# Keys of the last 1024 tokens in the second attention as Strassen products, with the token product's block sums moved later

## Chip, cores and metric

The kernel runs on one core of a Trainium2 chip. The metric is the device time in microseconds of one execution. TensorE is called PE below, VectorE DVE, ScalarE ACT, GpSimd POOL, and SyncE, whose queue issues most of the DMAs, SP.

## What is computed

Two kinds of layers alternate, twice, each with a residual connection: linear attention (A) and a gated feed-forward (B).

```python
x = x + A(layernorm(x)); x = x + B(layernorm(x))     # then both once more, same weights
# A: 2048 tokens, width D = 1024, 32 heads of 32
q, k, v = split(x @ wqkv)
phi = lambda t: where(t > 0, t + 1, exp(t)) + 1e-6
kv  = einsum("bhsd,bhse->bhde", phi(k), v)
den = einsum("bhqd,bhd->bhq", phi(q), phi(k).sum(s)) + 1e-6
o   = (einsum("bhqd,bhde->bhqe", phi(q), kv) / den) @ wo
# B: F = 3584
out = (relu(x @ W_gate) * (x @ W_up)) @ W_down
```

## The kernel before

**Tokens and quarters.** The 2048 tokens are 16 tiles of 128 (`ST`), in four quarters of `QT` = 4 tiles; `NS` = 8 tiles are one half. A layernormed tile is transposed by DMA into `xnT[l, quarter]`, which feeds the projections. Matmuls are 128 by 128 by 512.

**Projections.** A unit (`k_unit`, `q_unit`) makes one tile's keys or queries in one half of the columns: 8 matmuls into a PSUM bank, then `phi`: two ACT operations (L407, L408) and a DVE join (L411) that reads the bank. A POOL operation (`k_sum`, L484) adds the finished keys onto a running sum.

**The token product.** The values are never computed token by token. `m_products` makes M = layernormed tokens, transposed, times phi(k), a 1024 by 1024 matrix summed over the tokens, and multiplies it by wv per head afterwards. It uses Strassen's method in Winograd's form: tokens and columns are halved, and seven products of 32 matmuls (four groups `j` of 8) take the place of eight. PE's order is `mx`, `mx`, `mv`, `my`, `mv`, `my`, `my`. The first two need no sums. The others need block sums of token blocks (`n1` to `n4`) and key blocks (`k1` to `k4`), each eight times, once for a pair of tiles; they are DVE operations of 128 by 512, all recorded at L516. The third product reads n1 and k1, the fourth n2 and k2, the fifth n4, the sixth n3 and k3, the last k4. After each group of the fourth product DVE adds two banks (L563, called the V adds here), and the fifth product accumulates on the result. n4 and k4 overwrite blocks that the second product reads.

In the first attention all 64 sums stand inside `m_products`, four to a tick. In the second, k1 to k3 follow each key tile of the last 1024 tokens, n1 to n3 each layernorm of such a tile, and n4 and k4 stand after the second product.

**The normaliser.** After the second product two matmuls with ones (L492) spread the key sum over the partitions. Then a chain per query tile runs: a POOL multiply (L684), a DVE reduce, add and reciprocal (L689 to L691), a POOL scale (L696), a DMA transpose of the queries. It starts 2 ticks after the second product in the second attention, 6 in the first, and steps every 2 or 3 ticks:

```python
later.at(2 if l else 6, lambda: z_chain(0))
...
V += [self.ps.tile([P, NW], F32, tag="a", name=f"mv{j}") for j in range(QT)]
```

**Query blocks.** The second attention's queries of the first 1024 tokens are Strassen products already (`q_blocks`, L641): 28 matmuls of seven 4-matmul products for a block of two tiles by both column halves, where the units would take 32. Each block is cut into four steps, and key units stand between them. The weight sums they need were made in the feed-forward before (`load_q`, `sums_q`) and put into DRAM (`tq`); the token sums come from `sums_x` (L1006 to L1009). Product 1 starts bank X, which is copied to Y; product 5 goes to a bank of `kvp` and is copied to an SBUF tile V; product 2 finishes X, product 6 adds to Y, and Z and V are sums of Y and V; 7, 3 and 4 finish the rest. Each of the four results goes through `phi`.

**Order of the work.** `_Later` counts ticks, one for each unit, step or product group, and runs helpers when they are due; that sets their place in program order. Most instructions are then ordered by a scheduler at compile time. In a stretch marked `manual_schedule`, which includes `m_products`, DVE and POOL keep program order. `LN_AT` holds the ticks of the layernorms of tiles 8 to 15. `_Ring` loads weights in a planned order (`plan_A`) through SP's queue. PSUM has four banks "a" (`ps`), two "b" (`ps3`) and two of `kvp`; weights, slabs, transposed tokens and the like share 16 SBUF buffers.

Of the kernel before, what the change touches and what calls it, by code (L numbers as in the profile page):

```python
# [14 lines left out]
P = 128  # L15
# [4 lines left out]

LN_AT = (4, 8, 12, 16, 32, 35, 38, 41)

# [70 lines left out]
class _Net:  # L93
    def __init__(self, tc, ctx, x_d, wqkv_d, wo_d, wg_d, wu_d, wd_d, out_d):
# [34 lines left out]
        self.td = self.spill.tile([P, self.U, 4, NW], F16, name="td")  # L129
        self.tq = [self.spill.tile([P, 8, NW], F16, name=f"tq{h}") for h in range(2)]  # L130
        self.later = _Later()
# [98 lines left out]
    def xn_home(self, layer, t):  # L230

        low = lambda t: self.x[t][:, 0:self.D // 2].bitcast(BF16)
        if layer == 0:
            h = low(t)
        elif t == 0:
            h = self.temp([P, self.D], BF16, name=f"xn{layer}_0")
        elif t < self.NS:

            h = low(t - 1)
        else:  # L240
            h = self.slab_of(layer, 2 * (t - self.NS))
        self.xn[layer, t] = h
        return h

    def pk_home(self, layer, t):
        if (layer, t) not in self.pk:
            if layer == 0:
                h = self.slab_of(layer, t)
            elif t < self.NS:
                h = self.xb[t]  # L250
            else:
                h = self.slab_of(layer, 2 * (t - self.NS) + 1)
            self.pk[layer, t] = h
        return self.pk[layer, t]
# [170 lines left out]
    def plan_A(self, l):  # L425
        D = self.D
        cols = {"k0": D, "k1": D + NW, "v0": 2 * D, "v1": 2 * D + NW, "q0": 0, "q1": NW}
        for n in ("k0", "k1", "v0", "q0", "q1", "v1", "o0", "o1") if l == 0 else (
                "k0", "k1", "q0", "q1", "t0", "t1", "v0", "v1", "o0", "o1"):
            if n[0] == "t":  # L430
                self.ring.add((l, n), lambda t, h=int(n[1]): self.nc.sync.dma_start(
                    out=t[:, :, :].bitcast(F16), in_=self.tq[h]))
            elif n[0] == "o":
                c = NW * int(n[1])
                self.ring.add((l, n), self.wo_v[:, :, c:c + NW])
            else:
                self.ring.add((l, n), self.wqkv_v[:, :, cols[n]:cols[n] + NW])

    def layer_A(self, l, last_ln):
# [30 lines left out]
        def k_unit(q, j, c, between=None):  # L470
# [3 lines left out]
            later.at(1 + (10 if self.phi_lag else 0), lambda: k_sum(t, slice(c * NW, (c + 1) * NW)))  # L474
            if l and t >= self.NS and c == H - 1:
                later.at(3, lambda: sums(t - self.NS, k1, k2, k3))

# [48 lines left out]

        def sums(i, *fs):
            for f in fs:
                f(i)

        def m_products(q_first):
# [7 lines left out]
            last_k = self.last_phi  # L539
            if l == 0:  # L540
                jobs = [(f, i) for fs in ((n1, k1), (n2, k2), (n3, k3), (n4,), (k4,))
                        for i in range(NS) for f in fs]
                for n, (f, i) in enumerate(jobs):
                    later.at(1 + n // 4, lambda f=f, i=i: self.behind(last_k, f, (i,)))

# [26 lines left out]
            V += [self.ps.tile([P, NW], F32, tag="a", name=f"mv{j}") for j in range(QT)]  # L572
            if l:
                for i in range(NS):
                    later.at(1 + i // 2, lambda i=i: sums(i, n4, k4))
            product(lambda i: part(i, 0), lambda i: part(i, 2), V, True, keep)
# [42 lines left out]

        def q_blocks():  # L620


            xa, xb = self.xnT[l, 0], self.xnT[l, 1]
            sa, sb = self.xs[l, 0]
            q0, q1, t0, t1 = (ring.get((l, n)) for n in ("q0", "q1", "t0", "t1"))
            t0, t1 = (t[:, :, :].bitcast(F16) for t in (t0, t1))
            A = {1: xa[:, 0:4], 2: xa[:, 4:8], 3: sb[:, 4:8], 4: xb[:, 4:8], 5: sa[:, 0:4],
                 6: sa[:, 4:8], 7: sb[:, 0:4]}
            B = {1: q0[:, 0:4], 2: q0[:, 4:8], 3: q1[:, 4:8], 4: t1[:, 0:4], 5: t0[:, 0:4],
                 6: t1[:, 4:8], 7: t0[:, 4:8]}  # L630
            for sc in range(2):
                a = self.slot(f"pq{l}_{sc}", [P, QT, D])
                for i in range(QT):
                    pq_of[sc, i] = a[:, i, :]

            def steps(j):
# [8 lines left out]
                def one():  # L645
                    S["X"] = self.ps.tile([P, NW], F32, tag="a", name=f"qx{j}")
                    mm(1, S["X"], True)
                    S["Y"] = self.ps3.tile([P, NW], F32, tag="b", name=f"qy{j}")
                    nc.scalar.activation(out=S["Y"], in_=S["X"], func=ACT.Copy)
                    v = self.kvp.tile([P, NW], F32, tag=f"kv{j % 2}", name=f"qv{j}")  # L650
                    mm(5, v, True)
                    S["V"] = self.temp(name="qm5")
                    nc.scalar.activation(out=S["V"], in_=v, func=ACT.Copy)

                def two():
                    mm(2, S["X"])
                    self.phi(S["X"], half(pq_of[0, j], 0))
                    mm(6, S["Y"])
# [3 lines left out]
                def three():  # L662
                    mm(7, S["Y"])
                    nc.vector.tensor_tensor(out=S["V"], in0=S["Y"], in1=S["V"], op=ALU.add)
                    self.phi(S["V"], half(pq_of[1, j], 1))
                    mm(3, S["Z"])
                    self.phi(S["Z"], half(pq_of[0, j], 1))

                def four():
                    mm(4, S["Y"])  # L670
                    self.phi(S["Y"], half(pq_of[1, j], 0))

# [158 lines left out]
        else:  # L831
            ring.load_to(ring.index((l, "t1")) + 1)
            for j in range(QT):
                later.at(1 + j, lambda j=j: self.sums_x(l, 0, j))
        for i in range(QT if l == 0 else self.NS, self.ST):
            at = 8 + 3 * (i - QT) if l == 0 else LN_AT[i - self.NS]
            self.ln_at(at, l, i, 2)
            if l:
                later.at(at + 2, lambda i=i: self.send_away(i))
                later.at(at + 8, lambda i=i: sums(i - self.NS, n1, n2, n3))  # L840
        if l == 0:
# [13 lines left out]
        else:  # L855
            run(first)
            k = iter(row_major(k_unit, 1) + row_major(k_unit, 2)[:1])
            Q = q_blocks()
            todo = [Q[0][0]]
            for j in range(QT):  # L860
                todo += [next(k), Q[j][1], next(k), Q[j][2], Q[j + 1][0] if j + 1 < QT else next(k), Q[j][3]]
            run(todo)
            run(row_major(k_unit, 2)[1:], row_major(q_unit, 2))
        for q in range(1, self.NQ - 1) if l == 0 else ():
# [3 lines left out]
            run(row_major(k_unit, q), row_major(q_unit, q))  # L868
        run(row_major(k_unit, self.NQ - 1))
        with self.tc.manual_schedule(engines={mybir.EngineType.DVE, mybir.EngineType.Pool}):  # L870
# [102 lines left out]

    def load_q(self):

        self.wq = [self.slot(f"wq{h}", [P, 2, 4, NW]) for h in range(2)]
        for h, t in enumerate(self.wq):
            for n in range(2):
                self.nc.sync.dma_start(out=t[:, n, :, :], in_=self.wqkv_v[:, 4 * h:4 * h + 4, n * NW:(n + 1) * NW])

    def sums_q(self, n):

        (b11, b12), (b21, b22) = ([t[:, n, :, :] for n in range(2)] for t in self.wq)
        f16 = lambda a: a.bitcast(F16)
# [3 lines left out]
        if n % 2:  # L988
            h = n // 2
            self.later.at(2, lambda: self.nc.sync.dma_start(  # L990
                out=self.tq[h], in_=self.wq[h][:, :, :, :].bitcast(F16).rearrange("p a k n -> p (a k) n")))

# [4 lines left out]
    def sums_x(self, l, c, j):  # L997

        if j == 0:
            self.xs[l, c] = [self.slot(f"s{l}_{c}_{i}", dtype=F16) for i in range(2)]  # L1000
        s, v = self.xs[l, c], self.nc.vector
        cols = slice(j * P, (j + 1) * P)
        x1, x2 = self.xnT[l, 2 * c], self.xnT[l, 2 * c + 1]
        a11, a12, a21, a22 = (x[:, h:h + 4, cols] for x in (x1, x2) for h in (0, 4))
        s1, s2, s3, s4 = (x[:, h:h + 4, cols] for x in s for h in (0, 4))
        v.tensor_tensor(out=s1, in0=a21, in1=a22, op=ALU.add)  # L1006
# [10 lines left out]
    def glu(self, l, c, u, hT):  # L1017

        nc, later = self.nc, self.later
        x1, x2 = self.xnT[l, 2 * c], self.xnT[l, 2 * c + 1]  # L1020
        sa, sb = self.xs[l, c]
        A = {1: x1[:, 0:4, :], 2: x1[:, 4:8, :], 3: sb[:, 4:8, :], 4: x2[:, 4:8, :],
             5: sa[:, 0:4, :], 6: sa[:, 4:8, :], 7: sb[:, 0:4, :]}
        W = {}
# [142 lines left out]
    def layer_B(self, l, final):  # L1167
# [6 lines left out]
        for c in range(2):  # L1174
# [3 lines left out]
            for u in range(self.U):  # L1178
# [13 lines left out]
                if not final and c == 1:  # L1192
                    if u == 2:
                        self.load_q()
                    if 3 < u < 8:
                        self.later.at(4, lambda n=u - 4: behind(self.last_put, lambda: self.sums_q(n)))
                if c == 0 and u == 1:
# [86 lines left out]
```

## Time and profile before

| | |
|---|---|
| median of 3 runs | 1464.21 us (1464.2 to 1464.26) |
| the profiled execution | 1463.99 us, span 1462.2 us |
| PE busy | 1456.2 us, 6943 matmuls |
| DVE, ACT, POOL busy | 856.1, 578.2, 285.1 us |
| second attention's matmuls, by the timeline | from 735.2 to 938.7 us |
| its query blocks beside key units | 749.0 to 789.6 us |
| its token product begins | 828.6 us |
| granted PE clock | 1.000 of full speed |

The span runs from the first to the last instruction. A matmul's record is longer than its share of PE, because matmuls overlap; distances between starts are the measure. A group's line gives its busy time and the mean time of one instruction. A timeline row gives start, duration, engine, line and operation, and in brackets the idle time before it with what ended it.

### The profile page before, as it was taken

Reading aid. Unit: us, or ns where it says so; the run is one execution under the profiler, and the core shown is the slowest. Engines: PE = TensorE matmul, PEld = TensorE weight load, DVE = VectorE, ACT = ScalarE, POOL = GpSimd, SP = SyncE. Lnnn points to the kernel's source line nnn. Section 1 sums busy time; section 2 is a strip of 40 time slices with the busy share of each in tenths; the row PEclk is TensorE's granted clock in tenths of the full one; section 3 lists DMA queues with packets and bytes.
Section 4 is the critical chain, followed back from the end, with each engine's and each line's share of the span. In section 5 each row is a group of like instructions: output and inputs, shape, how many; then the busy total and the mean of one; then the engine's idle time right before and its main releaser. Section 6 shows DMA issues by size and latency. Waiting matters only on the chain.

```text
span 1462.2 us, 18717 instructions
## 1 busy us (share of the span) xinstructions
PE 1456.2 (100%) x6943; PEld 661.6 (45%) x6943; DVE 856.1 (59%) x1512; ACT 578.2 (40%) x1035; POOL 285.1 (19%) x190
## 2 busy tenths in 40 slices
PE   9999999999999999999999999999999999999999
PEld 4444444444444444444444444444444444444444
DVE  7978698666584444455388665776346433333632
ACT  6772564333340333340068626634333203333200
POOL 1354851011100011110033476401110001111000
PEclk9999999999999999999999999999999999999999
DMA  9840797564559956435942119975444787444461
GB/s 283 234 160 9 180 220 203 185 218 161 206 167 256 345 191 223 151 127 194 290 116 50 38 37 300 233 243 167 145 144 151 186 265 246 147 147 149 150 202 43
DMA packets 321195, 261.80 MB, mean 179 GB/s; under 512 B 105936, under 2 KB 293712, under 8 KB 319696
## 3 DMA queue, kind: packets, MB, share of 16 engines
q1 hardware_dynamic: 310096, 239.31, 55.8%
q10 hardware_dynamic: 11008, 21.30, 4.0%
q8 instruction: 54, 0.88, 0.2%
q14 instruction: 37, 0.30, 0.1%
HBM read 199.23 MB, written 36.70 MB: 161 GB/s over the span
## 4 chain that ended last, share of the span: by engine, by line
PE 96%; DVE 2%; ACT 1%; issue 0%; DMA 0%; DVEq 0%
PE ps L465 13%; PE dy L1132 10%; PE yg L1033 10%; PE yu L1033 10%; PE dv L1132 7%; PE dx L1132 7%; PE xg L1033 6%; PE xu L1033 6%; PE ps L732 4%; PE zu L1033 3%; PE zg L1033 3%; PE vu L1033 3%; PE vg L1033 3%; PE my L549 3%; PE mv L549 2%; PE mx L549 2%
## 5 line engine op out<-in xcount | busy, mean ns | idle before, releaser
L1033 PEld LDWEIGHTS <-w 128*128 128x128 f16 (+1 forms) x3136 | 306.7, 98 | 371.3 <-issue 1.4
L1086 POOL TENSOR_TENSOR h<-m5u,m5g 128x512 f16<-128x512 f32 x56 | 71.9, 1285 | 810.0 <-DVE m5u L1082 770.4
L465 PE MATMUL ps<-w,xnT 128*128 128x512 bf16 x896 | 197.5, 379 | 0.2 <-ACT xnT L325 0.2
L1132 PEld LDWEIGHTS <-h 128*128 128x128 f16 x1120 | 109.5, 98 | 132.2
L1069 DVE TENSOR_TENSOR zg<-yg,m5g 128x512 f32<-128x512 f32 x56 | 39.2, 699 | 188.9 <-PE yg L1033 188.9
L465 PEld LDWEIGHTS <-xnT 128*128 128x128 bf16 x896 | 86.9, 98 | 104.9 <-issue 1.6
L1033 PE MATMUL yg<-s,w 128*128 128x512 f16 x448 | 115.0, 379 | 0.1
L1033 PE MATMUL yu<-s,w 128*128 128x512 f16 x448 | 115.0, 379 | 0.0
L1033 PE MATMUL xg<-xnT,w 128*128 128x512 f16 x448 | 115.0, 379 | 0.0
L1033 PE MATMUL xu<-xnT,w 128*128 128x512 f16 x448 | 115.0, 379 | 0.0
L1041 ACT ACTIVATE m5g<-m5g 128x512 f32<-128x512 f32 x56 | 35.2, 629 | 189.2 <-DVE m5g L1082 185.4
L1132 PE MATMUL dy<-w,h 128*128 128x512 f16 x448 | 98.0, 379 | 0.0
L1132 PE MATMUL dx<-w,h 128*128 128x512 bf16 x448 | 97.3, 379 | 0.0
L408 ACT ACTIVATE e<-e,eps 128x512 f32<-128x512 f32 x128 | 91.6, 721 | 3.6
L684 POOL TENSOR_TENSOR kvc<-pq,kvc 128x1024 f32<-128x1024 bf16 x32 | 73.6, 2300 | 61.7 <-DVE den L689 37.6
L732 PE MATMUL ps<-T,pqT 128*128 128x512 bf16 x384 | 83.6, 379 | 0.0
L407 ACT ACTIVATE e<-ps 128x512 f32<-128x512 f32 x112 | 66.1, 590 | 37.9 <-PE ps L465 37.1
L1050 ACT ACTIVATE m5g<-vg 128x512 f32<-128x512 f32 x56 | 33.4, 597 | 110.9 <-PE vg L1033 85.2
L484 POOL TENSOR_TENSOR kvc<-kvc,slab 128x512 f32<-128x512 f32 x46 | 58.6, 1279 | 73.8 <-DVE slab L411 73.6
L1044 DVE TENSOR_TENSOR h<-yu,r 128x512 f16<-128x512 f32 x56 | 38.7, 691 | 56.0 <-PE yu L1033 56.0
L1082 DVE TENSOR_TENSOR m5u<-yu,m5u 128x512 f32<-128x512 f32 x56 | 38.7, 691 | 52.0 <-PE yu L1033 52.0
L1132 PEld LDWEIGHTS <-e 128*128 128x128 f16 x448 | 43.9, 98 | 52.8
(175 smaller groups left out, 2036.5 us busy)
## 6 DMA issues: line engine op xcount, KB each, us to landing
w<-in_B_W_gate_dram SPq DMA_DIRECT2D x56, 512.0 KB, 6.0
w<-in_B_W_up_dram SPq DMA_DIRECT2D x56, 512.0 KB, 5.2
w<-td SPq DMA_DIRECT2D x32, 896.0 KB, 4.7
w<-in_B_W_down_dram SPq DMA_DIRECT2D x24, 896.0 KB, 5.6
w<-tg SPq DMA_DIRECT2D x42, 512.0 KB, 7.0
w<-tu SPq DMA_DIRECT2D x42, 512.0 KB, 5.7
w<-in_A_wqkv_dram SPq DMA_DIRECT2D x9, 1024.0 KB, 7.8
away<-x SPq DMA_DIRECT2D x16, 512.0 KB, 5.4
```

The source lines that it names most:

```text
L407: nc.scalar.activation(out=e, in_=ps, func=ACT.Relu, scale=-1.0)
L408: nc.scalar.activation(out=e, in_=e, func=ACT.Exp, scale=-1.0, bias=self.eps6[:, 0:1])
L465: nc.tensor.matmul(by_row(ps), lhsT=self.xnT[l, l_q][:, kt, j * P:(j + 1) * P], rhs=w[:, kt, :].rearrange("p (b i d) -> p i b d", i=R, d=H ...
L484: nc.gpsimd.tensor_tensor(out=ksum[:, cols], in0=ksum[:, cols], in1=pk, op=ALU.add)
L549: nc.tensor.matmul(banks[j], lhsT=A(i)[:, j * P:(j + 1) * P], rhs=B(i), start=start and i == 0, stop=i == NS - 1, skip_group_check=True)
L684: nc.gpsimd.tensor_tensor(out=prod, in0=pq_of[sc, j], in1=zrow, op=ALU.mult)
L732: nc.tensor.matmul(ps, lhsT=pqT[sc][:, g, j * P:(j + 1) * P], rhs=T[g // 4][:, g % 4, n2 * NW:(n2 + 1) * NW], start=(g == 0), stop=(g == G ...
L1033: nc.tensor.matmul(ps, lhsT=W[w][m][:, k, :], rhs=A[m][:, k, :], start=start and k == 0, stop=k == 3, skip_group_check=True)
L1044: self.last_put = nc.vector.tensor_tensor(out=h[:, b, :], in0=ps, in1=R.pop(b), op=ALU.mult)
L1069: self.last_z = nc.vector.tensor_tensor(out=Z[w], in0=Y[w], in1=V[w], op=ALU.add)
L1086: nc.gpsimd.tensor_tensor(out=h[:, 3, :], in0=V["u"], in1=V["g"], op=ALU.mult)
L1132: nc.tensor.matmul(banks[j], lhsT=A(k)[:, j * P:(j + 1) * P], rhs=w[:, i, :], start=start and k == 0, stop=k == self.U - 1, skip_group_che ...
```

## The change

- The keys of tiles 8 to 15 (`first` = 2) are made by Strassen blocks: `q_blocks` becomes `blocks(p, first)`. The four key blocks run in two pairs, the two blocks of a pair step by step in turns. For keys, V is copied by DVE, Y by DVE in every second block, product 5 always goes to bank kv0, and the third block's Y lies in kv1.
- The weight sums for the keys are made like those for the queries: `load_w` and `sums_w` for both, in units 0 to 2 and 3 to 5 of the second half of the first feed-forward, two sums to a unit. Two more DRAM tiles hold them, and the ring has two loads more (`tk0`, `tk1`).
- The query units of tiles 8 to 11 come ahead of all keys of tiles 8 to 15. The token sums of those tiles (`sums_x(l, 1, j)`) are put into the x tiles 8 to 11, which have been stored away by then.
- Since n and k sums use the same x tiles, all 64 block sums now stand inside `m_products`, as in the first attention. The normaliser's start is left as it was.
- The layernorms of tiles 12 to 15 come earlier, with their transposes held back until the query blocks have freed a buffer. A slab holds tokens or keys of four tiles, where it held both of two.

```diff
-LN_AT = (4, 8, 12, 16, 32, 35, 38, 41)
+LN_AT = ((4, 2), (8, 2), (12, 2), (16, 2), (20, 12), (23, 10), (26, 8), (29, 6))
...
-                "k0", "k1", "q0", "q1", "t0", "t1", "v0", "v1", "o0", "o1"):
+                "k0", "k1", "q0", "q1", "tq0", "tq1", "tk0", "tk1", "v0", "v1", "o0", "o1"):
...
-            if l and t >= self.NS and c == H - 1:
-                later.at(3, lambda: sums(t - self.NS, k1, k2, k3))
...
-            if l == 0:
-                jobs = [(f, i) for fs in ((n1, k1), (n2, k2), (n3, k3), (n4,), (k4,))
-                        for i in range(NS) for f in fs]
-                for n, (f, i) in enumerate(jobs):
-                    later.at(1 + n // 4, lambda f=f, i=i: self.behind(last_k, f, (i,)))
+            jobs = [(f, i) for fs in ((n1, k1), (n2, k2), (n3, k3), (n4,), (k4,))
+                    for i in range(NS) for f in fs]
+            for n, (f, i) in enumerate(jobs):
+                later.at(1 + n // 4, lambda f=f, i=i: self.behind(last_k, f, (i,)))
...
-            if l:
-                for i in range(NS):
-                    later.at(1 + i // 2, lambda i=i: sums(i, n4, k4))
...
+            def put(src, q, j, n):
+                t = (first + q) * QT + j
+                cols = slice(n * NW, (n + 1) * NW)
+                self.phi(src, (pq_of[first + q, j] if p == "q" else self.pk_home(l, t))[:, cols])
+                if p == "k":
+                    later.at(1, lambda: k_sum(t, cols))
...
-                    S["Y"] = self.ps3.tile([P, NW], F32, tag="b", name=f"qy{j}")
-                    nc.scalar.activation(out=S["Y"], in_=S["X"], func=ACT.Copy)
-                    v = self.kvp.tile([P, NW], F32, tag=f"kv{j % 2}", name=f"qv{j}")
+                    if p == "k" and j == 2:
+                        S["Y"] = self.kvp.tile([P, NW], F32, tag="kv1", name=f"qy{j}")
+                    else:
+                        S["Y"] = self.ps3.tile([P, NW], F32, tag="b", name=f"qy{j}")
+                    copy(S["Y"], S["X"], p == "k" and j % 2)
+                    v = self.kvp.tile([P, NW], F32, tag=f"kv{j % 2 if p == 'q' else 0}", name=f"qv{j}")
                     mm(5, v, True)
                     S["V"] = self.temp(name="qm5")
-                    nc.scalar.activation(out=S["V"], in_=v, func=ACT.Copy)
+                    copy(S["V"], v, p == "k")
...
             if l:
                 later.at(at + 2, lambda i=i: self.send_away(i))
-                later.at(at + 8, lambda i=i: sums(i - self.NS, n1, n2, n3))
...
-            k = iter(row_major(k_unit, 1) + row_major(k_unit, 2)[:1])
-            Q = q_blocks()
+            k = iter(row_major(k_unit, 1))
+            Q = blocks("q", 0)
             todo = [Q[0][0]]
             for j in range(QT):
-                todo += [next(k), Q[j][1], next(k), Q[j][2], Q[j + 1][0] if j + 1 < QT else next(k), Q[j][3]]
-            run(todo)
-            run(row_major(k_unit, 2)[1:], row_major(q_unit, 2))
+                todo += [next(k), Q[j][1], next(k), Q[j][2]] + ([Q[j + 1][0]] if j + 1 < QT else []) + [Q[j][3]]
+            q2 = row_major(q_unit, 2)
+            run(todo[:-1] + q2[:1] + todo[-1:])
+            later.at(1, lambda: ring.load_to(ring.index((l, "tk1")) + 1))
+            self.xs[l, 1] = [self.x[self.NS + i][:, :].bitcast(F16).rearrange("p (a n) -> p a n", n=NW)
+                             for i in range(QT)]
+            for j in range(QT):
+                later.at(4 + j, lambda j=j: self.sums_x(l, 1, j))
+            run(q2[1:])
+            K = blocks("k", 2)
+            run([K[j + i][n] for j in (0, 2) for n in range(4) for i in range(2)])
...
-        run(row_major(k_unit, self.NQ - 1))
+        if l == 0:
+            run(row_major(k_unit, self.NQ - 1))
...
-                    if u == 2:
-                        self.load_q()
-                    if 3 < u < 8:
-                        self.later.at(4, lambda n=u - 4: behind(self.last_put, lambda: self.sums_q(n)))
+                    if u in (0, 3):
+                        self.load_w("qk"[u // 3])
+                    if u in (1, 2, 4, 5):
+                        for n in range(2):
+                            self.later.at(4 + 5 * n, lambda w="qk"[u // 4], n=2 * (u % 3 - 1) + n: behind(
+                                self.last_put, lambda: self.sums_w(w, n)))
```

## The prediction

> **What bounds the kernel now.** I read the page's busy times first, then its chain, then the busy times by stage of the second attention.
>
> ```profile
> span 1462.2 us, 18717 instructions
> PE 1456.2 (100%) x6943; PEld 661.6 (45%) x6943; DVE 856.1 (59%) x1512; ACT 578.2 (40%) x1035; POOL 285.1 (19%) x190
> PE 96%; DVE 2%; ACT 1%; issue 0%; DMA 0%; DVEq 0%
> ```
> ```profile
> 749.00:789.60 40.60, 40.56 (x189) 18.30 (x188) 31.11 (x58) 35.26 (x64) 13.79 (x12) 1.00 0.12 24
> 828.60:842.40 13.80, 13.80 (x65) 6.23 (x64) 5.03 (x9) 6.37 (x10) 2.85 (x3) 1.00 0.00 0
> 842.40:870.50 28.10, 28.10 (x132) 12.74 (x130) 18.18 (x35) 6.35 (x11) 21.44 (x10) 1.00 0.20 38
> ```
> The stage columns are stretch, length, then busy us of PE, PEld, DVE, ACT, POOL. TensorE idles nowhere here: 64 key matmuls start from 735.21 to 749.02, 215.8 ns apart. A matmul taken away is worth 216 ns; any wait that reaches PE is a pure loss. ACT is at 87% beside the query blocks; DVE has only 5.03 of 13.80 us of work in the token product's first two products.
>
> The first attention already makes all block sums inside its token product. DVE's and POOL's timelines there:
>
> ```profile
> 106.87 0.41 DVE L516 TENSOR_TENSOR x<-x,x 128x512 f16<-128x512 bf16 x1
> 107.20 1.38 DVE L516 TENSOR_TENSOR x<-slab 128x512 f16<-128x512 bf16 x1
> 108.51 0.41 DVE L516 TENSOR_TENSOR x<-x,x 128x512 f16<-128x512 bf16 x1
> 120.41 5.58 POOL L684 TENSOR_TENSOR kvc<-pq,kvc 128x1024 f32<-128x1024 bf16 x1 [12.11 <-ACT kvc L494]
> 127.83 0.70 DVE L563 TENSOR_TENSOR mv<-my,m 128x512 f32<-128x512 f32 x1 [3.82 <-PE my L549]
> 128.44 1.42 DVE L516 TENSOR_TENSOR x<-x 128x512 f16<-128x512 bf16 x4
> 135.59 1.22 DVE L689 TENSOR_REDUCE den<-kvc 128x32 f32<-128x1024 f32 x1
> ```
> And in the second attention:
>
> ```profile
> 844.37 4.21 POOL L684 TENSOR_TENSOR kvc<-pq,kvc 128x1024 f32<-128x1024 bf16 x1 [11.90 <-ACT kvc L494]
> 848.62 1.22 DVE L689 TENSOR_REDUCE den<-kvc 128x32 f32<-128x1024 f32 x1 [2.02 <-POOL kvc L684]
> 851.79 0.70 DVE L563 TENSOR_TENSOR mv<-my,m 128x512 f32<-128x512 f32 x1 [1.34 <-PE my L549]
> 830.03 2.45 POOL L484 TENSOR_TENSOR kvc<-kvc,slab 128x512 f32<-128x512 f32 x2 [1.03 <-DVE slab L411]
> ```
> See three things. A POOL operation and a block sum exclude each other (0.41 becomes 1.38). The normaliser multiply (L684, else 2.12) takes 5.58 and 4.21: it got in only when the run of sums ended. And DVE obeys program order: in the second attention the first reduce stands ahead of the V adds (L563), in the first behind all sums.
>
> **What the Trainium skill says.** "SBUF — State Buffer", section "Who interferes with whom": a DVE instruction with two SBUF inputs contends with a GpSimd instruction that reads SBUF; one holds the port for its whole instruction, the other blocks. The rows above agree; that the waiting multiply loses to eleven later sums is the trace's own. "TensorE: Matmul & The Clock Gate", section "Wait — 56ns, not 53.3ns?": 215.7 ns per warm 512-column matmul; the trace has 215.8.
>
> **The change part by part.** T is the end of the last key matmul (828.6 now).
>
> *Matmuls.* Eight token tiles by two halves by 8 are 128; four blocks by 7 products by 4 are 112. 16 x 0.2158 = **3.45 us less**, on the path.
>
> *Two chains of key blocks.* Both chains put product 5 in one bank, kv0. From one chain's last such matmul to the other's first lie four matmuls, 0.86 us. The DVE copy must fit: matmul tail 0.16, copy about 0.66 (nearest row: the PSUM join, 0.69), two hand-overs of 0.03: 0.88. A join ahead of it (0.61 pitch) makes the wait 0.3 to 0.5. At the change of pairs ACT owes six phis of 1.24 (0.61 and 0.63 pitch), 7.4 us, for what PE makes in 5.2; the third block's Y copy queues behind, and product 2 waits for it, some 0.8. I sum 0.3 + 0.5 + 0.8, and let other matmuls fill the first: **1.3 lost**; bounds 0 (all filled) and 2.5 (V joins, two SBUF inputs, also blocked by POOL's key sums).
>
> *The last join.* ACT starts those six phis for the second pair at T-3.4 (product 7 ends T-4.2, V add 0.7). They end at T+4.0, the last join at T+4.85. Today it ends at 830.92, T+2.3.
>
> *The block sums.* 48 sums (n1 to n3, k1 to k3) start there: 48 x 0.336 = 16.1, plus about 2.0 behind the last two key sums on POOL. The run ends at T+22.9. Its products are safe: n1, k1 are done by T+12, needed T+14.2; n2, k2 by T+17.5, needed T+21.2.
>
> *The normaliser.* Its delay stays 2 ticks. POOL's multiply comes at T+15.8, gets in after the run: done T+25.0 (if it slips in earlier, the run ends 2.1 later, and the reduce comes out the same). Reduce, add, reciprocal (848.62 to 850.44) take 1.8: T+26.8. Only now comes the first V add, ready at T+23.2 today; done T+27.4. Behind it are n4 0-3, V add, n4 4-7, second reduce, V add, k4 0-3, V add. The second multiply holds the port from T+26.3 to T+28.4, then the first scale (1.91) takes turns with the n4 sums. Product five needs all eight n4 in its first group, due T+28.05 to T+29.8; the last is done at T+33.0 to T+33.6, so 3.5 to 4.1 are lost. The second reduce delays the third V add, a third multiply holds k4 0-3, and the fourth V add is done at T+38.5 to T+40.9: 1.9 to 3.6 more. Together 5.4 or 7.7, by whether the sums or the scale go first; I take **6.5 lost**, lower bound 2, upper 8. The multiplies catch up afterwards, so the folds (886.43 now) shift with PE only.
>
> *Beside other work, at nothing.* (1) Four more weight sums of 1.22 in the second half of the first feed-forward: DVE is busy 4.8 of 12 us there; were that cover gone, one sum ahead of an add would cost some 0.4. (2) On SP's queue the first weight load moves from 497.2 to near 485, among gate and up loads at a DMA share of 1.03. The next of these, issued at 484.9 now, comes some 6 us later (2 MB at 335 GB/s) and lands near 500; PE wants it near 507. The load itself lands near 495 (8 us), its first sum stands near 497: 2 us in hand. (3) Two 1 MB loads more on SP, between token transposes: 7.8 us to landing as the query pair had, while six query units give 10.4; their buffers and four more come from six that the query blocks free. Two later transposes queue behind (3.2 each); the second pair needs them, some 12 us on. The four stores of x tiles move to a stretch where SP has only transposes. If (2) or (3) fail, DVE waits in order for a DMA: 0 to 3 us. (4) Layernorms of tiles 12 to 15 move into the query blocks: 4 x 0.5 us of ACT, while some 15 block sums leave DVE. (5) 16 sums of token blocks, 0.36 each, on DVE in the last four query units: 1.4 + 0.6 for a join against 1.73 of PE per unit, so DVE is at most about 1 us late at the first key block; the two early V copies would pay for it, within the 2.5 above. (6) Spare x tiles as their buffers, other slabs: no instruction.
>
> **Sum.** -3.45 + 1.3 + 6.5 = +4.35. The profiled run is 1463.99 (span 1462.2 and 1.8 around it), 0.22 below the median 1464.21; on the median that is 1468.5. Likeliest's own range: 1465.5 to 1471.5.
>
> **Rivals.**
> *No collision (faster).* If DVE can start the first V add by T+24.2, nothing is lost: in the first attention it starts at T+23.15, and product five follows with 1.0 in hand. That asks for a run ending by T+20.3, so for a last join near T+2.3 and a free POOL. For: the first attention makes the same sums with no PE idle. Against: there the normaliser waits 6 ticks, and ACT's six phis are not there. Then 1464.2 - 3.45 + 0 to 1.3 = 1460.8 to 1462.1.
> *A starved key sum.* If the last key sum meets a running series, it waits as the multiply does, until T+22; PE's two ones matmuls, due T+13.8, then stand about 7 to 10 us, while part of the later loss vanishes: +8.6 + 1.3 - 3.45, about 1470.7. Against: in the 830.03 row POOL went in after one sum.
> *Late transfers.* Parts (2) and (3), 2 us on top: 1470.5.
> *Not what it says.* If TensorE still issues 128 key matmuls, only losses stay: about 1466 to 1472.
>
> **How the numbers follow.** Likeliest 0.55 (slower 0.42, within 0.13), no collision 0.25 (faster 0.14, within 0.11), starved 0.08 (slower), late transfers 0.10 (slower 0.07, within 0.03), not as said 0.02. So faster 0.14, within 0.2% 0.28, slower 0.58; 0.2%, 2.9 us, is about what a measurement of this kernel can tell from no change. Range 1461.0 to 1473.0.
>
> **What would show it.** PE: 112 key-block matmuls in place of 128, idle of about a microsecond at the change of pairs. DVE: 48 sums in one run ending near T+23; the first L689 about T+25; the first V add at T+26.8, no longer T+23. PE idle before the second mv product, ended by DVE, in pieces of 3.5 to 4 and 2 to 3.5 us. Wrong, if the V adds come by T+24 or the mv product starts without idle; wrong in size, if the key blocks idle over 2.5 us.

## The result, and the profile after

The changed kernel takes **1470.51 us** (median of 4 runs, 1470.1 to 1471.3) against 1464.2 us for the kernel before on the same chip: ratio 1.0044, 95% interval 1.0026 to 1.0061. It is 6.3 us slower. The profiled execution took 1470.4 us, its span is 1468.3, 6.1 longer than before; the differences below are made against this span. T, the end of the last key matmul, is 827.30 here.

The page's head, with the busy times and the chain's shares:

```profile
span 1468.3 us, 18717 instructions
PE 1456.5 (99%) x6927; PEld 660.3 (45%) x6927; DVE 872.9 (59%) x1546; ACT 577.5 (39%) x1037; POOL 287.1 (20%) x190
PE 93%; DVE 3%; DMA 1%; ACT 1%; POOL 1%; issue 0%; SPq 0%; DVEq 0%; ACTq 0%; POOLq 0%
```

Sixteen matmuls are gone (6927 for 6943), yet PE's busy time has not fallen and the span has grown. In the chain PE falls from 96% to 93%, DVE rises from 2% to 3%, and DMA and POOL come in with 1% each. What PE waits for in the second attention, where the same question had no row before (waited for: us in total, times, longest):

```profile
PE mv L542 <- DVE slab L514: 2.7, 3, 1.7
PE mv L542 <- DVE mv L556: 1.8, 1, 1.8
PE qv L644 <- DVE qm L635: 0.9, 1, 0.9
PE fold L726 <- DMA w<-in_A_wo_dram: 0.8, 1, 0.8
```

The first two rows are the token product's fifth product, waiting for its n4 blocks and then for the last V add; the third is the change of pairs in the key blocks; the fourth a wait for a weight load behind the token product. Lines have moved: the block sums are now L514, the V adds L556, the normaliser's multiply, reduce and scale L690, L695 and L702.

By stage (stretch, length, busy us of PE, PEld, DVE, ACT, POOL, then PE's granted clock, the DMA share and GB/s): the key blocks, the first two products, the third to the fifth, and 3.4 us cut out of these.

```profile
801.80:827.30 25.50, 24.50 (x114) 10.92 (x113) 20.71 (x35) 17.38 (x30) 12.04 (x11) 1.00 0.20 63
827.30:841.50 14.20, 14.20 (x67) 6.47 (x66) 13.19 (x27) 8.68 (x16) 6.61 (x6) 1.00 0.12 36
841.50:869.30 27.80, 23.36 (x97) 9.72 (x96) 25.65 (x53) 5.56 (x10) 17.51 (x5) 0.94 0.10 20
860.00:863.40 3.40, 3.40 (x10) 1.28 (x10) 3.33 (x7) 0.60 (x1) 1.60 (x1) 0.54 0.09 20
```

The third row carries the result: before, that stage was full of matmuls (132 in 28.10 us), now it has 97. DVE, with 5.03 us of work in the first two products before, has 13.19: the run of sums. The last row is a surprise: a stretch where PE is busy all the time with only 10 matmuls, at a clock of 0.54. The matmuls there start 0.43 us apart in place of 0.216. (A single one's record is 0.38 us long at full clock, so the starts are what to compare.)

DVE's timeline in the fifth product (start, duration, operation; in brackets the idle time before and what ended it):

```profile
849.80 0.41 DVE L514 TENSOR_TENSOR x<-slab,x 128x512 f16<-128x512 bf16 x1
852.23 1.22 DVE L695 TENSOR_REDUCE den<-kvc 128x32 f32<-128x1024 f32 x1 [2.02 <-POOL kvc L690]
853.97 0.67 DVE L556 TENSOR_TENSOR mv<-my,m 128x512 f32<-128x512 f32 x1
854.55 4.10 DVE L514 TENSOR_TENSOR slab<-slab,x 128x512 f16<-128x512 bf16 x4
858.57 0.69 DVE L556 TENSOR_TENSOR mv<-my,m 128x512 f32<-128x512 f32 x1
...
862.82 4.11 DVE L514 TENSOR_TENSOR slab<-slab,x 128x512 f16<-128x512 bf16 x4
866.84 0.69 DVE L556 TENSOR_TENSOR mv<-my,m 128x512 f32<-128x512 f32 x1
```

and POOL's:

```profile
843.03 9.17 POOL L690 TENSOR_TENSOR kvc<-pq,kvc 128x1024 f32<-128x1024 bf16 x1 [8.19 <-ACT kvc L492]
853.53 2.12 POOL L690 TENSOR_TENSOR kvc<-pq,kvc 128x1024 f32<-128x1024 bf16 x1 [1.33 <-DVE den L695]
855.61 2.08 POOL L702 TENSOR_TENSOR pq<-pq,den 128x1024 bf16<-128x1024 bf16 x1
```

Read them as one story. The run of 48 sums lasts from 831.63 to 850.2. The multiply of 843.03 stands through 21 sums that start after it and ends after the last. The reduce behind it comes at T+24.9, and the first V add at T+26.7. Then the second multiply and the first scale hold the port while four n4 sums take 4.10 us, which in a quiet stretch take 1.41. With the second reduce the same happens to k4, and the fourth V add ends at T+40.2. From the distances of PE's starts, the idle is 3.42 us ahead of the fifth product's groups, 1.93 ahead of its last one, and the low clock costs another 1.7.

In the key blocks, DVE's timeline at the change of pairs:

```profile
815.06 1.49 DVE L411 SCALAR_TENSOR_TENSOR slab<-qm,e 128x512 bf16<-128x512 f32 x1 [0.92 <-ACT e L408]
816.47 0.68 DVE L411 SCALAR_TENSOR_TENSOR slab<-qz,e 128x512 bf16<-128x512 f32 x1
817.07 0.68 DVE L635 COPY qm<-qv 128x512 f32<-128x512 f32 x1
```

The V join, whose two inputs are both in SBUF, takes 1.49 in place of 0.69, since a key sum runs on POOL (813.61 to 816.0). The copy that frees bank kv0 stands behind it, and PE idles 1.07 us; with 0.26 at the change before, 1.33 in all.

Two smaller places. In the first feed-forward four gaps of 0.15 to 0.17 us are new (at 502.6, 514.9, 539.2 and 551.4), 0.64 in all. DVE there:

```profile
500.75 1.22 DVE L1004 TENSOR_TENSOR wq<-wq,wq 128x2048 f16<-128x2048 bf16 x1
501.88 0.69 DVE L1087 TENSOR_TENSOR zu<-yu,m5u 128x512 f32<-128x512 f32 x1
502.48 0.68 DVE L1100 TENSOR_TENSOR m5g<-yg,m5g 128x512 f32<-128x512 f32 x1
```

The second weight sum of a unit stands ahead of the adds that PE's next bank waits for. Last, SP's queue behind the token product, where the wo load (L40) follows the query transposes:

```profile
857.72 29.46 SPq L711 DMA_TRANSPOSE pqT<-pq  x6
887.29 0.52 SPq L40 DMA_DIRECT2D w<-in_A_wo_dram  x1
```

It is issued at 887.29, 8.8 us later than before (878.47), while PE was ready for the fold only 5.7 us later. The gap there is 0.95, before 0.26.

The sum: -3.45 (matmuls) + 1.33 (key blocks) + 0.64 (feed-forward) + 7.04 (fifth product: 3.42 + 1.93 + 1.7) + 0.69 (fold) + 0.2 (the start of the kernel 0.36, which differs from one execution to the next, less a gap of 0.20 in the query blocks that is gone) = +6.4, against 6.1 of span. The 0.3 between them comes back behind the fold, at a place that stays open.

### The profile page after: what moved, and what is told of

The parts are those of the page before. It is cut to its first block, busy times and chain, and to the rows that moved or that the text cites. A ratio compares the mean times of both kernels' runs of the same rounds, so it can differ in the third digit from the quotient of the medians.

```text
span 1468.3 us, 18717 instructions
## 1 busy us (share of the span) xinstructions
PE 1456.5 (99%) x6927; PEld 660.3 (45%) x6927; DVE 872.9 (59%) x1546; ACT 577.5 (39%) x1037; POOL 287.1 (20%) x190
## 4 chain that ended last, share of the span: by engine, by line
PE 93%; DVE 3%; DMA 1%; ACT 1%; POOL 1%; issue 0%; SPq 0%; DVEq 0%; ACTq 0%; POOLq 0%
PE ps L465 11%; PE dy L1150 10%; PE yu L1051 10%; PE yg L1051 10%; PE dx L1150 7%; PE dv L1150 7%; PE xg L1051 6%; PE xu L1051 6%; PE ps L738 4%; PE zg L1051 3%; PE zu L1051 3%; PE vu L1051 3%; PE vg L1051 3%; PE my L542 2%; PE mx L542 2%; PE qy L644 1%
## 5 line engine op out<-in xcount | busy, mean ns | idle before, releaser
L465 PE MATMUL ps<-w,xnT 128*128 128x512 bf16 x768 | 170.1, 379 | 0.5 <-DMA w<-in_A_wqkv_dram 0.3
L465 PEld LDWEIGHTS <-xnT 128*128 128x128 bf16 x768 | 74.3, 98 | 90.5 <-issue 1.7
L690 POOL TENSOR_TENSOR kvc<-pq,kvc 128x1024 f32<-128x1024 bf16 x32 | 78.5, 2452 | 60.1 <-DVE den L695 39.7
L407 ACT ACTIVATE e<-ps 128x512 f32<-128x512 f32 x96 | 56.6, 590 | 34.1 <-PE ps L465 33.6
```

What stands on the lines that cost most here:

```text
L407: nc.scalar.activation(out=e, in_=ps, func=ACT.Relu, scale=-1.0)
L465: nc.tensor.matmul(by_row(ps), lhsT=self.xnT[l, l_q][:, kt, j * P:(j + 1) * P], rhs=w[:, kt, :].rearrange("p (b i d) -> p i b d", i=R, d=H ...
L690: nc.gpsimd.tensor_tensor(out=prod, in0=pq_of[sc, j], in1=zrow, op=ALU.mult)
```

## Experiments

The theory: the loss in the fifth product is one of order on DVE. The block sums moved later, the normaliser did not, so its first reduce gets between the run and the V adds. Rivals: the run's length alone (48 sums and a late last join) delays the V adds, with or without the normaliser; or the key blocks, through their late last join and the key sums on POOL, carry most of it.

**The normaliser 6 ticks after the second product in both attentions.**

```diff
-            later.at(2 if l else 6, lambda: z_chain(0))
+            later.at(6, lambda: z_chain(0))
```

> The changed kernel with one number changed: the normaliser of the second attention starts 6 ticks after the second product, not 2. Nothing is left out. Theory A (the first reduce stands ahead of the V adds in DVE's order, and POOL's multiplies and scale take the port from n4 and k4): the V adds come at T+23 to T+29 again, no idle in the fifth product, no half clock behind it; about 7 us less than the changed kernel, 1463.4. The fold's wait for wo goes too, since fewer transposes stand ahead of that load on SP's queue: 1462.8 to 1463.8. Theory B (the 48 sums are too late by themselves, because the key blocks' last join is late): n4 is still late, at most 2 us come back, 1468.5 or more. Theory C (the later normaliser is paid for at the folds or the outputs): new idle there, 1465 or more.

Measured: 1463.0 us (1462.42 to 1465.3, 12 runs) against 1464.07, ratio 0.9994 (0.9986 to 1.0003). DVE's timeline there:

```profile
849.84 0.70 DVE L556 TENSOR_TENSOR mv<-my,m 128x512 f32<-128x512 f32 x1 [0.23 <-PE my L542]
850.45 2.43 DVE L514 TENSOR_TENSOR slab<-slab,x 128x512 f16<-128x512 bf16 x4
852.81 0.68 DVE L556 TENSOR_TENSOR mv<-my,m 128x512 f32<-128x512 f32 x1
854.75 0.68 DVE L556 TENSOR_TENSOR mv<-my,m 128x512 f32<-128x512 f32 x1
855.35 1.41 DVE L514 TENSOR_TENSOR slab<-slab,x 128x512 f16<-128x512 bf16 x4
856.69 0.68 DVE L556 TENSOR_TENSOR mv<-my,m 128x512 f32<-128x512 f32 x1
858.63 1.20 DVE L695 TENSOR_REDUCE den<-kvc 128x32 f32<-128x1024 f32 x1
```

The first V add starts as soon as PE has its group, the other three follow 2 to 3 us apart, and the reduce comes after all four. The run of sums is as long as it was, and the multiply is starved just the same (9.17 us), but nobody who matters waits for it. The stage is full again:

```profile
841.50:869.30 27.80, 27.80 (x131) 12.63 (x129) 24.58 (x57) 5.56 (x10) 18.56 (x6) 1.00 0.06 12
```

One number takes away all 7.04 us of the fifth product, so the run's length alone is not the cause. The number moves two things at once, the reduce in DVE's order and POOL's hold of the port. By the timelines, with T at 826.69 here, the last n4 sum ends at T+28.1 in place of T+33.3: 3.5 of these 5.2 us are the first V add (T+23.1, not T+26.7) and 1.7 the first four n4 sums (2.43, not 4.10). What either would cost alone no run shows. What the edit did not do, against the expectation, is help the fold:

```profile
PE fold L726 <- DMA w<-in_A_wo_dram: 1.5, 1, 1.5
PE qv L644 <- DVE qm L635: 0.9, 1, 0.9
```

The wait for wo has grown, from 0.8 to 1.5. PE reaches the fold earlier, while the load is still issued only when the first quarter's transposes have landed.

**The late block sums alone.** The kernel before with all 64 sums inside the token product, and key units as they were.

```diff
-            if l and t >= self.NS and c == H - 1:
-                later.at(3, lambda: sums(t - self.NS, k1, k2, k3))
...
-            if l == 0:
-                jobs = ...
+            jobs = ...
...
-            if l:
-                for i in range(NS):
-                    later.at(1 + i // 2, lambda i=i: sums(i, n4, k4))
...
-                later.at(at + 8, lambda i=i: sums(i - self.NS, n1, n2, n3))
```

> The kernel before with only the move of the block sums: all 64 of the second attention inside the token product as in the changed kernel; key units, layernorm ticks and normaliser (2 ticks) as before. Nothing is left out. Theory A: last join near T+2.3, run of sums to about T+19.6, first reduce near T+21.7, first V add near T+23.5, so barely late; but the second multiply and the first scale still take the port from n4: 2 to 5 us slower than before, 1466 to 1469. Theory B (only the key blocks make them late): within 1 us of before, 1464 to 1465. If it costs as much as in the changed kernel (7 us), the key blocks' late join adds nothing.

Measured: 1468.74 us (1467.94 to 1469.21, 5 runs), ratio 1.0033 (1.002 to 1.0046), so 4.7 us slower without a single key block. PE's waits and DVE's rows:

```profile
PE mv L546 <- DVE mv L560: 2.9, 2, 2.7
```
```profile
849.56 1.22 DVE L683 TENSOR_REDUCE den<-kvc 128x32 f32<-128x1024 f32 x1 [2.02 <-POOL kvc L678]
851.36 0.70 DVE L560 TENSOR_TENSOR mv<-my,m 128x512 f32<-128x512 f32 x1
851.97 4.01 DVE L514 TENSOR_TENSOR slab<-slab,x 128x512 f16<-128x512 bf16 x4
```

It is the same picture, some 2.6 us earlier: the run of sums starts at 830.41 where the key blocks have it at 831.63, and one of its sums is held by a key sum on POOL, not three. T is 828.21 here, so the first V add comes at T+23.1 and is on time; n4 comes almost in time (idle 0.56 in three pieces), and only the last V add is late: 2.89 us. A stretch of low clock follows here too and costs 1.7. By the distances of starts the stage loses 5.1 us; the medians show 4.7, and this execution reached T 0.4 earlier than the profile before. So the loss has two parts: the late sums, with the normaliser left at its place, cost 5.1 us by themselves, and the key blocks add the other 1.9 of the 7.04.

**The key blocks without their key sums.** 16 POOL operations less; the normaliser lacks the keys of the last 1024 tokens.

```diff
-                if p == "k":
-                    later.at(1, lambda: k_sum(t, cols))
```

> The changed kernel without the 16 key sums of the key blocks on POOL (the normaliser then lacks the last 1024 tokens). Tests what makes the 0.9 us wait at the change of pairs. Theory A (a key sum on POOL holds up the V join, 1.49 where a free one takes 0.69, and with it the V copy that frees kv0): V joins 0.69, wait at the change of pairs 0.3 or less, and the run of block sums starts about 0.3 earlier and ends 2 to 3 us earlier since no key sum holds its first sums; the fifth product's idle falls by 2 to 3 us. Theory B (ACT's Y copy or the chain of four matmuls sets it): the wait stays at 0.7 to 0.9.

Measured: 1467.64 us in one run. The V join takes 0.69 again:

```profile
814.98 0.69 DVE L411 SCALAR_TENSOR_TENSOR slab<-qm,e 128x512 bf16<-128x512 f32 x1 [0.92 <-ACT e L408]
```

so the key sums do make the 1.49. But the gap at the change of pairs falls only from 1.07 to 0.77, now in two pieces: 0.28 for the copy out of kv0 and 0.49 for the Y copy, which still stands behind the phis on ACT. The POOL sums are 0.3 of that wait. Of the rest, 0.49 is ACT's backlog, and 0.28 is DVE's copy, behind two joins of which the first had waited 0.92 for ACT. The idle of the fifth product is 4.6 us here, 0.7 less than in the changed kernel and not the 2 to 3 less of the expectation; no low clock follows it, and that, 1.7, is most of the 2.9 us that this kernel gains.

**Three mends together.** Six ticks as above; in every second key block product 5 comes ahead of product 1; and the weight sums of the feed-forward one to a unit.

```diff
-            later.at(2 if l else 6, lambda: z_chain(0))
+            later.at(6, lambda: z_chain(0))
...
+                    early = p == "k" and j % 2 == 0
+                    if early:
+                        five()
...
-                    if u in (0, 3):
-                        self.load_w("qk"[u // 3])
-                    if u in (1, 2, 4, 5):
-                        for n in range(2):
-                            self.later.at(4 + 5 * n, lambda w="qk"[u // 4], n=2 * (u % 3 - 1) + n: ...
+                    if u in (0, 5):
+                        self.load_w("qk"[u // 5])
+                    if u in (1, 2, 3, 4, 6, 7, 8, 9):
+                        self.later.at(4, lambda w="qk"[u // 5], n=u % 5 - 1: ...
```

> The changed kernel with three edits: normaliser at 6 ticks; in the first chain of each pair of key blocks product 5 issued ahead of product 1, so that eight matmuls and not four lie between the two uses of kv0; weight sums one to a unit at tick 4 (units 1 to 4 and 6 to 9, key weights loaded in unit 5). Nothing is left out. If the three losses are what I read (7 us at the fifth product with its half clock and the fold, 1.3 at the key blocks, 0.64 in the feed-forward), their sum leaves 3.45 us below before plus a start that varies by some tenths: 1460.8 to 1461.8. If the key blocks' wait comes from ACT or the V adds instead, 1462 to 1463. If a second set of late sums on DVE holds up the second pair, more.

Measured: 1462.85 us (1462.04 to 1463.47, 12 runs), ratio 0.9991 (0.9982 to 1.0). The four gaps in the feed-forward are gone, which confirms their cause. The key blocks' gaps are unchanged, 0.26 and 1.07, so the distance of the two matmul groups that share kv0 does not set them. That idea fell; the queue of DVE and ACT is what is left, and fits. The 1460.8 to 1461.8 of the expectation was missed by the 1.33 us of these gaps and by the fold, which still waits 0.9 for wo.

**Five ticks instead of six** (weight sums spread, key blocks as in the changed kernel).

```diff
-            later.at(2 if l else 6, lambda: z_chain(0))
+            later.at(5 if l else 6, lambda: z_chain(0))
```

> The changed kernel with the second attention's normaliser 5 ticks after the second product (2 in the changed kernel) and the weight sums spread over eight units, one to each. The edits on the key blocks stay. Theory A (what counts is only that the first reduce comes behind the run of 48 sums and does not hold the V adds; and the fold waits because the first wo load needs the buffer of the first quarter's queries, which is free only when its four transposes have landed, so an earlier normaliser gives an earlier fold): the V adds keep their places with at most 1 us of idle in front of the fifth product, and the wait for wo shrinks from 1.5 us (6 ticks) to 0.3 or less; 1461.5 to 1462.5 against 1464.1 before. Rival (a reduce that comes a tick earlier gets between two V adds and holds the fifth product's groups again): idle of 1 to 3 us before the fifth product, 1463 to 1465.

Measured: 1464.11 us (1463.18 to 1465.59, 13 runs) against 1464.25, ratio 0.9998 (0.9989 to 1.0006).

```profile
PE fold L726 <- DMA w<-in_A_wo_dram: 1.4, 1, 1.4
PE my L542 <- DVE mt L556: 0.6, 1, 0.6
```

The fifth product has no idle, though the reduce now stands between the third and the fourth V add. The fold gained nothing: the first scale is 2.5 us earlier, but the third multiply (863.78, with six ticks 863.86) waits for the reduce behind the k4 sums, and from there on (867.73, with six ticks 867.80) the chain is where it was. The wo load leaves at 880.13, with six ticks at 880.03. The expectation failed because it moved the chain's start and took the rest to follow.

**The wo load ahead of the transposes** (six ticks, weight sums spread).

```diff
+            if l:
+                ring.load_to(ring.index((l, "o0")) + 1)
             z_row()
...
-                if j == 1:
+                if l == 0 and j == 1:
                     ring.load_to(ring.index((l, "o0")) + 1)
```

> As the variant with the normaliser after 6 ticks and the weight sums spread, but the first load of wo is issued on SP ahead of the first quarter's query transposes and no longer behind them, into another buffer. Theory (the wait of 1.0 to 1.5 us at the fold is the wo load queued behind those transposes, whose buffer it takes): the load lands some 10 us earlier, the wait at the fold is gone, 1461.3 to 1462.3. Rival 1 (the wo load takes a buffer that the first transposed queries then lack): the transposes start later, the output units wait for them, slower by 2 to 8 us. Rival 2 (the fold waits for something else, the last token product's results or wv): wo lands early and the fold starts at the same distance from the last product, 1462.5 to 1463.

Measured: 1465.66 us (1464.8 to 1469.16, 21 runs), ratio 1.001 (1.0004 to 1.0017): slower. The profiled execution is the longest of the 21, 1469.16: its matmuls start 0.43 us apart until 14.2 us, where in the profile before that ends at 5.2, and T comes at 830.54, with three mends at 826.99. That accounts for the 3.5 us that it has over the median; the waits below lie behind T, and all times in it are late by about as much. DVE and POOL there:

```profile
874.45 0.69 DVE L556 TENSOR_TENSOR mt<-my,m 128x512 bf16<-128x512 f32 x1 [6.28 <-PE kv L498]
```
```profile
876.35 2.12 POOL L692 TENSOR_TENSOR kvc<-pq,kvc 128x1024 f32<-128x1024 bf16 x1 [4.66 <-DVE den L697]
```

The load was issued at 829.00, but an add that writes a part of M (`mt`) waits 6.28 us for PE's matmuls of the next step, the third reduce stands behind it on DVE, POOL's multiply waits for that, and the second half of wo leaves only at 893.56; PE waits 1.7 for it at a later fold. This is the first rival in another place: a buffer seems to be missing, and not the transposes lack it (they start on time) but `mt`. That it is the buffer is my reading of the wait, since a semaphore row names only who came last; no run took it apart.

**Five ticks and the early wo load together** (weight sums spread).

> The two edits together: normaliser 5 ticks after the second product in the second attention, the first load of wo ahead of the transposes, weight sums spread. If both theories hold, one of the two is enough for the fold, and this is within 0.5 us of the better one: 1461.3 to 1462.3. If the transposes lack a buffer, the earlier normaliser does not help, since the buffer comes free with the token product, and it is as slow as the other.

Measured: **1462.56 us** (1462.17 to 1463.51, 13 runs) against 1464.25, ratio 0.9988 (0.998 to 0.9996). Its only wait of PE in the second attention, and SP's row:

```profile
PE qv L646 <- DVE qm L637: 0.9, 1, 0.9
```
```profile
825.04 0.37 SPq L40 DMA_DIRECT2D w<-in_A_wo_dram  x1
```

The fold's wait is gone. The wait of `mt` is still there, but only 1.89 us, and nothing on PE's path stands behind it. The expectation that this would equal the better of the two single edits failed in its reason, and by 0.3 us in its range: neither edit alone is faster than the kernel before (1464.11 and 1465.66). It is the fastest kernel of this study, 1.7 us below the one before by medians. Its span is 1.8 below, and what it gets from the matmuls and keeps is 3.45 less 1.33 in the key blocks, 2.1.

**The changed kernel again, and the one without key sums again**, both for the low clock.

> The changed kernel without any edit, profiled a second time. It asks whether the half clock of 3.41 us behind the idle of the fifth product belongs to the kernel or to the single execution. If it follows from the length of the idle, it is there again at the same place, and the time is 1470.1 to 1471.3 in all runs. If it depends on where the idle falls against something that the kernel does not set, this profile may lack it, and the runs fall into two groups some 1.5 us apart.

Measured: 1470.2 us (1469.73 to 1471.68, 5 runs), ratio 1.0041 (1.0028 to 1.0053). The low clock is there again at the same place, with a mean clock of 0.999 in all five runs:

```profile
841.50:869.30 27.80, 22.86 (x97) 9.69 (x97) 25.65 (x53) 5.53 (x10) 17.52 (x5) 0.94 0.10 20
860.00:863.00 3.00, 3.00 (x9) 1.08 (x9) 2.93 (x7) 0.60 (x1) 1.23 (x1) 0.53 0.08 18
```

> The changed kernel without the 16 key sums of the key blocks on POOL (its normaliser lacks the keys of the last 1024 tokens), a second time and timed in rounds. Its first profile had 4.6 us of PE idle around the fifth product, more than the 3.4 us of the kernel with the late sums alone, and still no stretch at half clock. If the half clock follows from the idle alone, it never comes in this kernel: clock 1.000 in all runs, 1467.4 to 1467.9. If it depends on where the idle falls against something that the kernel does not set, some of its runs have a clock of 0.999 and are 0.8 to 1.5 us longer than the others.

Measured: 1467.73 us (1467.05 to 1469.7, 9 runs), ratio 1.0026 (1.0016 to 1.0036). Six runs have a clock of 1.000 and take 1467.05 to 1468.24; three have 0.998 or 0.999 and take 1468.66, 1469.56 and 1469.7, on average 1.7 us more. In the kernel with the late sums alone one run of five is at 1.000, and it is the shortest (1467.94; the others 1468.67 to 1469.21). So the same kernel does or does not meet the low clock, at 0.9 to 1.7 us, where the starts give 1.6 to 1.7. Of the runs without a trace only the mean clock is on record, not the place: single runs of kernels with no idle in the fifth product have 0.999 too, one of 41 of the kernel before (1466.54), one of 12 with six ticks (1465.3) and one of 13 with five (1465.59).

## Why the prediction was right, and where its sizes were off

The side and the mechanism were right; the value was 2.0 us low.

- *Matmuls, -3.45.* 16 fewer, as counted.
- *Key blocks, +1.3.* Measured 1.33. The parts differ: the 0.26 at the first shared bank was not filled by other matmuls, as I had assumed. The change of pairs costs 1.07, where I had added 0.5 and 0.8. The V join held by POOL's key sum, which I had only in the upper bound, is real and 0.3 of it. That the sum fits so well is luck: one part was 0.26 too low and the other 0.23 too high.
- *The last join at T+4.85.* It ends at T+4.4. ACT's six phis do set it.
- *The run of sums, to T+22.9; the reduce at T+25.0; the first V add at T+26.8.* Measured T+22.9, T+24.9 and T+26.7. The starved multiply, read from the first attention's row of 5.58, was the key to these; here it stood 9.17. (The sums that started after it there are ten by the timeline, not eleven.)
- *The fifth product, +6.5 from 5.4 or 7.7.* The last n4 ends at T+33.3 (T+33.0 to T+33.6 forecast), the fourth V add at T+40.2 (T+38.5 to T+40.9). The idle is 3.42 + 1.93 = 5.35, the lower of the two cases. This step failed on something that it lacked: PE came out of the idle at half its clock and lost another 1.7. With it the stage costs 7.04.
- *No collision.* It named six ticks in the first attention, and ACT's six phis that are not there, as the reasons why the same sums do no harm. The run with six ticks here has the phis, and six ticks are enough: without the reduce in between, V adds on time and no idle. Its kernel took 1463.0, where the rival had 1460.8 to 1462.1; the two points on (1) and on the folds are of the size of the difference.
- *A starved key sum.* Not met: PE's two ones matmuls start at 841.11, T+13.8, when they are due.
- *Costed at nothing, (1).* The four extra weight sums cost 0.64. The cover was counted as busy time over the stretch (4.8 of 12 us), but DVE obeys order: the second sum of a unit came just ahead of an add. My price for a lost cover, 0.4 for one, was paid four times at 0.16.
- *"The folds shift with PE only."* Wrong by 0.7. The multiplies do not catch up ahead of the wo load: it waits on SP behind transposes whose time the normaliser sets.
- *(2) to (6).* No wait of PE for the loads, transposes and token sums of these points shows in the trace of after.

Of the 2.0 us, 1.7 is the clock, 0.64 the weight sums, 0.69 the fold and 0.2 the start of the kernel; 1.15 less idle than taken stands against them, so that the total came as near as 2.0 is in part luck.

Two pages of the Trainium skill bear on this. "SBUF — State Buffer", section "Who interferes with whom", says that issue order decides which of DVE and GpSimd blocks. The trace agrees for single operations (the V join of 1.49 behind a key sum), not for a run: the multiply of 843.03 was passed by 21 sums that started after it. "TensorE: Matmul & The Clock Gate", section "What's actually happening", says that PE falls to half clock after an idle window of about 3.4 us, that the window runs freely, and that PE needs a busy one to come back. The measured clock of 0.53 to 0.54, its length of some 3 to 3.4 us, and the mean clock of 1.000 in six of nine runs of one kernel agree, and so does the grid of 3.413 us told in the last section. But the longest single piece of idle was 1.83 us in the first profile of the changed kernel and 2.69 in the second, so a window that is not wholly idle was enough here.

## What to carry to other kernels

When work is moved later on an engine that runs in program order, move what waits for it, and what is queued between it and its reader, by the same amount: here one delay of 2 ticks left at its place cost 7.04 us, twice the 3.45 that the saved matmuls gave. Cover is to be counted at the place in the order where the added instruction stands, not over a stretch, and a stall of TensorE is to be priced with a possible slow start behind it. A weight load that takes a buffer from a chain is as late as the chain: ask of each load which buffer it takes and who frees it.

## What was not expected of the hardware

- A POOL multiply with SBUF inputs stood 9.17 us (else 2.12) through 21 DVE additions of 0.41 us, one behind the other every 0.335. In the kernel with the late sums alone it was 5.58. The wait is as long as the run that it meets.
- In three traces 3.4 to 3.6 us of idle in pieces on PE was followed by 3.41 us at half clock, which cost 1.6 to 1.7 us; in the two without key sums 4.6 us was not. The traces show what may tell them apart. The granted clock changes on a grid: from its first rise to full speed at 6.36 us to its fall at 859.69 the changed kernel's trace has 853.33 us, 250 times 3.413, and the distances in the other traces are whole multiples too. In the one step of the grid ahead of the fall PE was busy for 1.21 us (in the second profile of the changed kernel 1.06, with the late sums alone 1.14). In the emptiest such step around the fifth product the two traces without key sums have PE busy for 1.47 and 1.51 us, and no fall follows. The changed kernel's step, and one of these two:

```profile
856.28:859.69 3.41, 1.21 (x5) 0.34 (x4) 3.41 (x6) 0.00 (x0) 1.42 (x1) 1.00 0.23 46
862.85:866.26 3.41, 1.47 (x7) 0.68 (x7) 3.41 (x9) 0.00 (x0) 0.33 (x1) 1.00 0.40 77
```

So it may be how much of the idle falls into one step. Where the grid lies differs between executions (the first rise comes between 4.4 and 6.6 us, in one at 14.2), which would make it a matter of chance. This was read from five traces afterwards; no run tested it, and why all nine runs of the changed kernel have a mean clock below 1.000 stays open.

- Ahead of PE's first transposes, where no kernel here has an edit, PE's idle is 0.88 us in the profile before, 0.47 in the changed kernel's, and up to 2.60 in the others. A difference of half a microsecond between two single profiles says nothing by itself.
